# Scores of the first four tiles as pairs of plain fp32 matmuls in the two row halves, from one q/k buffer a tile

## The chip, the cores and the metric

The kernel runs on one core of a Trainium2 chip. The metric is the device time of one execution in microseconds: for the kernel before, a median of 612.29 us over three runs (611.9 to 612.41). The engines are TensorE (PE, its weight loads PEld), VectorE (DVE), ScalarE (ACT), GpSimd (POOL) and SyncE (SP, which here only issues transfers). PSUM has eight banks; matmuls write there, DVE and ACT read it.

## The reference

An mLSTM attention (a recurrence over 768 steps, 2 batches, 8 heads of 40) feeds a mixture of four dense experts and then a gated second layer:

```python
for t in range(S):
    m_new = np.maximum(f_gate[:, :, t] + m, i_gate[:, :, t])
    f_stab = np.exp(f_gate[:, :, t] + m - m_new)
    i_stab = np.exp(i_gate[:, :, t] - m_new)
    C = f_stab * C + i_stab * einsum('bhd,bhe->bhde', vt, kt)
    n = f_stab * n + i_stab * kt
    y[:, :, t] = sigmoid(o_gate[:, :, t]) * (C @ qt) / max(abs(n @ qt), 1.0)
x = y.transpose(0, 2, 1, 3).reshape(B * S, H * D)
out = sum over e of p[:, e] * (relu(x @ w1[e]) @ w2[e])        # moe
final = ((out @ w_a) * (out @ w_b)) @ w_out                    # moe2
```

## The kernel before

The recurrence is cut into chunks of 128 steps, which makes 12 tiles (6 chunks j by 2 batches b, tile n = 2j + b). For each tile, `scores` (L508) makes the products k.q of eight heads, four to a PSUM bank `pt_c` (halves hh = 0 and 1); `weights_of` (L485) makes the exponents of the decay weights in a bank `pt_a`; `w_exp` (ACT, L497) and `w_mask` (POOL, L505) turn them into the weights w; `s1b` (DVE, L517) multiplies w with `pt_c`; `s2a` (L527) multiplies the result with the values into `pt_y`, and from chunk 1 on a second product with the old state goes into `pt_i` (L533). `s2b` (L543, L546) and `s2x` (L556 to L562) make the tile's output x on DVE, `s3a` (L145 to L147) transposes it, and its two float32r parts `xh` and `xl` feed the experts. `state` (L583, `pt_u`) and `state_in` (L591) make the new state.

For tiles 0 to 3 (NP = 4) the scores are plain fp32 matmuls. Each half has a buffer of 120 rows by 1024; rows 0 to 63 of tiles 0 and 1 (40 rows for tiles 2 and 3, which go into the buffers of tiles 0 and 1) are loaded, rows 64 to 119 are zeroed once (`zero_qk`, L337, two on DVE and two on POOL), and the matmul contracts all 120 rows. A plain fp32 matmul stands in the trace as two weight loads and two matmul records. Later tiles split q and k into float32r parts (`split_qk`, `low_qk`).

The experts' matmuls are float32r. In the first 200 us a stream of `Item`s (L208, L287 to L289) is interleaved with the recurrence; from 202 us on `quad_a` (L228) and `quad_b` (L253) run alone, with 64-row matmuls in the two row halves of the array.

The order on each engine is written out by hand: the list `ev` holds (time, function, arguments), sorted by that number, and each engine runs its instructions in that order. The four banks of the pool `ps_t` (4 to 7 in the built program) go in turn to `pt_c`, `pt_y`, `pt_i`, `pt_x`, `pt_u`, `pt_e` and some `pt_a`, in the order in which the code asks for them; the first matmul into a bank waits for the last reader of what was there.

Of the kernel before, what the change touches and what calls it, by code (L numbers as in the profile page):

```python
# [48 lines left out]
def mlstm_moe_kernel(ctx, tc, gates, qk, qc, kvo, dp, w1b, w2b, ident_d, bdmask_d, rsel_d, exp_d, out):  # L49
    nc = tc.nc  # L50
# [254 lines left out]
    ps_b = ctx.enter_context(tc.tile_pool(name="ps_b", bufs=2, space=PS))  # L305
    with ExitStack() as c1:
        cq = ExitStack()
        qp = cq.enter_context(tc.tile_pool(name="qp", bufs=2, side="right"))
# [670 lines left out]
```

## Time and profile before

| | us |
|---|---|
| median of three runs | 612.29 |
| profiled execution, first to last instruction (its span) | 609.3 |
| median less span: what lies around the span | 3.0 |
| PE busy in the span | 598.1 (98%) |
| DVE, ACT, POOL busy | 406.5, 277.9, 193.3 |
| scores of tiles 0 to 3, 64 matmul records | 8.2 busy, 6.49 to 39.9 |

The profiled execution's own time is not given apart from its span; with the 3.0 us around the span it stands for the median. The granted clock is 1.00 in every stretch listed. In the timeline rows matmul ends are modelled, so the step from one start to the next is what counts. Times in the rows are from the span's start.

### The profile page before, as it was taken

The numbers are of one execution on the slowest core, as the hardware profiler recorded it, in microseconds if no ns is written. First come the engines' busy times: TensorE is split into PE (matmuls) and PEld (weight loads), VectorE is DVE, ScalarE is ACT, GpSimd is POOL, SyncE is SP. The second block draws the span as 40 slices with busy tenths as digits, with TensorE's granted clock in tenths as the row PEclk, the third lists the DMA queues.
The fourth block names the chain that finished last, engine by engine and source line by source line (L and its number), as shares of the span: only waits on it lengthen the run. The fifth ranks groups of instructions, "written<-read, shape, count | busy, mean of one in ns | idle before, by whom it ended". The sixth has DMA issues, their size and how long they took to land.

```text
span 609.3 us, 14397 instructions
## 1 busy us (share of the span) xinstructions
PE 598.1 (98%) x5815; PEld 564.5 (93%) x5815; DVE 406.5 (67%) x829; ACT 277.9 (46%) x643; POOL 193.3 (32%) x233
## 2 busy tenths in 40 slices
PE   8799999999999999999999999999999999999997
PEld 5699999999999899999999999988898988888886
DVE  6898868676553333333789899898776787864344
ACT  7687476756533323333344344454553434331211
POOL 5486426363501011334233333333222222310000
PEclk9999999999999999999999999999999999999999
DMA  8877463737202122222222222222111120200002
GB/s 247 214 219 202 128 181 103 197 104 200 58 19 64 39 62 80 72 75 79 56 76 69 63 75 56 59 63 65 47 50 45 38 56 20 60 16 1 2 31 100
DMA packets 29351, 51.63 MB, mean 85 GB/s; under 512 B 3485, under 2 KB 18117, under 8 KB 29285
## 3 DMA queue, kind: packets, MB, share of 16 engines
q1 hardware_dynamic: 15925, 26.32, 15.9%
q10 hardware_dynamic: 12448, 22.03, 13.2%
q0 software_dynamic: 912, 2.36, 1.4%
q8 instruction: 45, 0.74, 0.5%
q14 instruction: 21, 0.17, 0.1%
HBM read 47.92 MB, written 2.00 MB: 82 GB/s over the span
## 4 chain that ended last, share of the span: by engine, by line
PE 92%; DVE 3%; POOL 1%; issue 1%; DMA 1%; ACT 1%; SPq 0%; DVEq 0%; POOLq 0%
PE psy L253 27%; PE psa L228 27%; PE psb L228 11%; PE psa L208 10%; PE psy L287 3%; PE psy L289 3%; PE psy L288 3%; PE pt_y L527 3%; PE pt_c L513 1%; PE pt_i L533 1%; POOL wl L93 1%; PE pt_u L583 1%; DMA acc<-in_w1b 1%; PE pt_x L145 0%; DMA gt<-in_gates 0%
## 5 line engine op out<-in xcount | busy, mean ns | idle before, releaser
L228 PE MATMUL psa<-xh,wh 64*128 64x512 f32 x576 | 135.2, 390 | 0.0
L253 PE MATMUL psy<-wl,hh 64*128 64x320 f32 x752 | 131.3, 305 | 0.0
L253 PE MATMUL psy<-wh,hh 64*128 64x320 f32 x752 | 131.3, 305 | 0.0
L253 PE MATMUL psy<-wh,hl 64*128 64x320 f32 x752 | 131.2, 305 | 0.0
L228 PE MATMUL psa<-xh,wl 64*128 64x512 f32 x414 | 97.4, 389 | 0.0
L253 PEld LDWEIGHTS psy<-wh,hh 64*128 64x128 f32 x752 | 85.7, 184 | 0.8
L228 PEld LDWEIGHTS psa<-xh,wh 64*128 64x128 f32 x576 | 80.9, 184 | 5.9 <-issue 0.9
L253 PEld LDWEIGHTS psy<-wl,hh 64*128 64x128 f32 x752 | 85.5, 184 | 0.8
L253 PEld LDWEIGHTS psy<-wh,hl 64*128 64x128 f32 x752 | 85.7, 184 | 0.0
L228 PE MATMUL psa<-xl,wh 64*128 64x512 f32 x384 | 85.6, 389 | 0.0
L828 DVE SCALAR_TENSOR_TENSOR hl<-psa,hh 128x512 fp32r<-128x512 f32 x60 | 38.6, 685 | 55.2 <-ACT hh L827 54.9
L125 POOL TENSOR_TENSOR wl<-tp,lf 128x272 fp32r<-128x272 f32 x48 | 38.8, 809 | 113.1 <-DVE tp L124 111.4
L228 PE MATMUL psb<-xh,wh 64*128 64x512 f32 x216 | 69.8, 389 | 0.0
L228 PEld LDWEIGHTS psa<-xh,wl 64*128 64x128 f32 x414 | 60.7, 184 | 3.7
L228 PE MATMUL psb<-xh,wl 64*128 64x512 f32 x180 | 58.5, 389 | 0.0
L228 PEld LDWEIGHTS psa<-xl,wh 64*128 64x128 f32 x384 | 55.2, 184 | 3.6
L122 POOL TENSOR_TENSOR lf<-lf,sq 128x272 f32<-128x272 f32 x48 | 38.1, 794 | 62.9 <-ACT wh L121 48.9
L276 DVE SCALAR_TENSOR_TENSOR hl<-psa,hh 128x256 fp32r<-128x256 f32 x72 | 30.3, 421 | 40.4 <-ACT hh L275 40.0
L93 POOL TENSOR_TENSOR wl<-raw,wh 128x352 fp32r<-128x352 f32 x28 | 26.4, 947 | 95.1 <-ACT wh L91 68.6
L275 ACT ACTIVATE hh<-psa 128x256 fp32r<-128x256 f32 x72 | 27.6, 383 | 59.2 <-PE psa L208 58.5
L827 ACT ACTIVATE hh<-psa 128x512 fp32r<-128x512 f32 x60 | 32.6, 596 | 44.7 <-PE psy L253 26.6
L208 PE MATMUL psa<-xh,wh 128*128 128x256 f32 x216 | 51.5, 293 | 0.3 <-ACT xh L133 0.3
(146 smaller groups left out, 1435.1 us busy)
## 6 DMA issues: line engine op xcount, KB each, us to landing
raw<-in_w2b ACTq DMA_DIRECT2D x48, 272.0 KB, 2.8
qk_t<-in_qk SPq DMA_DIRECT2D x16, 480.0 KB, 4.7
raw<-in_w1b ACTq DMA_DIRECT2D x32, 176.0 KB, 2.3
acc<-in_w1b SPq DMA_DIRECT2D x24, 176.0 KB, 4.0
kvo_t<-in_kvo SPq DMA_DIRECT2D x10, 364.5 KB, 7.1
Rr<-dL_t ACTq DMA_DIRECT2D x5, 512.0 KB, 6.3
og_t<-in_kvo SPq DMA_DIRECT2D x6, 320.0 KB, 4.6
out<-acc SPq DMA_DIRECT2D x12, 160.0 KB, 1.9
```

What stands on the lines that cost most here:

```text
L93: lo_eng.tensor_tensor(wl[:, cs], raw, wh[:, cs].bitcast(F32), op=ALU.subtract)
L122: nc.gpsimd.tensor_tensor(lf, lf, sq, op=ALU.mult)
L125: nc.gpsimd.tensor_tensor(wl[:, cs], tf, lf, op=ALU.add)
L208: nc.tensor.matmul(ps, l, r, start=(i == 0), stop=(i == len(prs) - 1))
L228: return nc.tensor.matmul(ps[g], w[rows, o:o + P], x, start=start, stop=stop)
L253: ms = [nc.tensor.matmul(ps[t], l[rows, t * P:(t + 1) * P], w[rows, off:off + DM], start=start, stop=stop) for t, rows in zip(two, (UP, DN))]
L275: nc.scalar.activation(self.hh, ps, AF.Relu)
L276: nc.vector.scalar_tensor_tensor(self.hl, ps, 0.0, self.hh.bitcast(F32), op0=ALU.max, op1=ALU.subtract)
L287: nc.tensor.matmul(ps, lh, wh[:, off:off + DM], start=(fi == 0), stop=False)
L288: nc.tensor.matmul(ps, lh, wl[:, off:off + DM], start=False, stop=False)
L827: nc.scalar.activation(hh, ps[f], AF.Relu)
L828: nc.vector.scalar_tensor_tensor(hl, ps[f], 0.0, hh.bitcast(F32), op0=ALU.max, op1=ALU.subtract)
```

## The change

One buffer a tile takes both halves: q and k of heads 0 to 3 in rows 0 to 47, of heads 4 to 7 in rows 64 to 111 (48 rows loaded each, for all four tiles; 40 are used). Tiles 0 to 2 take the three buffers `qk`, tile 3 one of the two `qs`, so no tile's load waits for another's scores. The zero fills go. `scores2` makes both halves of a tile in one piece, alternating between the row halves, each matmul with 40 rows.

```diff
         def load_qk(n, hh, eng=None):
             t = td.setdefault(n, {})
-            if 2 <= n < NP:
-                t["qk", hh] = td[n - 2]["qk", hh]
+            if n < NP:
+                if "two" not in t:
+                    tag, bufs = ("qs", 2) if n == NP - 1 else ("qk", QB)
+                    t["two"] = qp.tile([KS, 2, 512], F32, tag=tag, name="qk_t", bufs=bufs)
+                at, r, to = 64 * hh, RQ, t["two"]
             else:
...
-            r = 64 if n < 2 else D if n < NP else KS
-            (eng or nc.sync).dma_start(v[0:r], qk[n, hh, 0:r])
-
-        def zero_qk(n, hh, eng):
-            eng.memset(td[n]["qk", hh][64:KS], 0.0)
+            (eng or nc.sync).dma_start(v[at:at + r], qk[n, hh, 0:r])
...
+        def scores2(n):
+            t = td[n]
+            for hh in range(2):
+                t["pc", hh] = ps_t.tile([P, 512], F32, tag="t", name="pt_c")
+            for h in range(4):
+                hs = slice(h * P, (h + 1) * P)
+                for hh in range(2):
+                    v = t["two"][64 * hh:64 * hh + D]
+                    nc.tensor.matmul(t["pc", hh][:, hs], v[:, 1, hs], v[:, 0, hs], start=True, stop=True, skip_group_check=True)
...
-            (-51.612, scores, 1, 0), (-51, weights_of, 1, 1, ps_b, "b"), (-51, w_exp, 1, 1), (-49.609, go, w1[0:1]), (-49.488, w_exp, 1, 0),
...
+            (-51.612, scores2, 1), (-51, weights_of, 1, 1, ps_b, "b"), (-51, w_exp, 1, 1), (-49.609, go, w1[0:1]), (-49.488, w_exp, 1, 0),
...
```

`scores2` stands where the first of a tile's two halves stood. On PE at tiles 0 and 1 there was, before:

```order
L513 MATMUL pt_c<-qk_t 128x128 [waits DMAHW2_49,DVE_49]
L513 MATMUL pt_c<-qk_t 128x128 x3
L513 MATMUL pt_c<-qk_t 128x128 [waits DMAHW3_49,DVE_49]
L492 MATMUL pt_a<-Rr_107,LT_105 128x512 [waits DVE_49]
L492 MATMUL pt_a<-Rr_107,LT_105 128x512 [waits Activation_49]
L492 MATMUL pt_a<-Rr_108,LT_105 128x512 [waits DVE_49]
L513 MATMUL pt_c<-qk_t 128x128 [waits DMAHW4_49,Pool_49]
L513 MATMUL pt_c<-qk_t 128x128 x3
L492 MATMUL pt_a<-Rr_108,LT_105 128x512 [waits Activation_49]
L513 MATMUL pt_c<-qk_t 128x128 [waits DMAHW5_49,Pool_49]
L527 MATMUL pt_y<-kvo_t,w_t 128x82 [waits DMAHW6_49,DVE_49]
```

and there is now, in the changed kernel's line numbers:

```order
L515 MATMUL pt_c<-qk_t 128x128 [waits DMAHW3_49]
L515 MATMUL pt_c<-qk_t 128x128 [waits DMAHW2_49]
L515 MATMUL pt_c<-qk_t 128x128 x6
L492 MATMUL pt_a<-Rr_107,LT_105 128x512 [waits DVE_49]
L492 MATMUL pt_a<-Rr_107,LT_105 128x512 [waits Activation_49]
L492 MATMUL pt_a<-Rr_108,LT_105 128x512 [waits DVE_49]
L515 MATMUL pt_c<-qk_t 128x128 [waits DMAHW4_49]
L515 MATMUL pt_c<-qk_t 128x128 [waits DMAHW5_49]
L515 MATMUL pt_c<-qk_t 128x128 x6
L492 MATMUL pt_a<-Rr_108,LT_105 128x512 [waits Activation_49]
L537 MATMUL pt_y<-kvo_t,w_t 128x82 [waits DMAHW6_49,DVE_49]
```

The last `pt_a` of tile 1 stood behind four matmuls of `pt_c` and now stands behind eight. On PE around the scores of tile 3 (`w_t_470` and `w_t_492` are tile 2's weights of half 0 and half 1, `pt_c_540` is tile 3's half 1, `pt_c_581` its half 0) there was, before:

```order
L513 MATMUL pt_c_540<-qk_t_128 128x128 [waits DMAHW4_49,Activation_49]
L513 MATMUL pt_c_540<-qk_t_128 128x128 x3
L583 MATMUL pt_u_547<-kvo_t_136,kw_t_431 120x123 [waits DVE_49]
L527 MATMUL pt_y_553<-kvo_t_251,w_t_470 128x82 [waits DMAHW5_49,DVE_49]
L527 MATMUL pt_y_553<-kvo_t_251,w_t_470 128x82 x3
...
L527 MATMUL pt_y_553<-kvo_t_251,w_t_492 128x82 [waits DVE_49]
L533 MATMUL pt_i_577<-cbd_t_519,qc_t_253 128x123 [waits DMAHW6_49]
L513 MATMUL pt_c_581<-qk_t_126 128x128 [waits DMAHW3_49,DVE_49]
L492 MATMUL pt_a_603<-Rr1_108,LT1_106 128x512 [waits DVE_49]
```

and there is now (`w_t_466` and `w_t_488` are tile 2's halves, `pt_c_536` and `pt_c_537` tile 3's):

```order
L515 MATMUL pt_c_536<-qk_t_244 128x128 [waits DMAHW3_49,Activation_49]
L515 MATMUL pt_c_537<-qk_t_244 128x128 [waits DMAHW4_49,DVE_49]
L515 MATMUL pt_c_536<-qk_t_244 128x128
L593 MATMUL pt_u_548<-kvo_t_131,kw_t_427 120x123 [waits DVE_49]
L537 MATMUL pt_y_554<-kvo_t_247,w_t_466 128x82 [waits DMAHW5_49,DVE_49]
L537 MATMUL pt_y_554<-kvo_t_247,w_t_466 128x82 x3
...
L537 MATMUL pt_y_554<-kvo_t_247,w_t_488 128x82 x4
L543 MATMUL pt_i_578<-cbd_t_515,qc_t_249 128x123 [waits DMAHW6_49,DVE_49]
L492 MATMUL pt_a_599<-Rr1_108,LT1_106 128x512 [waits DVE_49]
```

The half-0 scores of tile 3 moved from behind `pt_i` to the front, so six tiles ask for banks in another order. In the built programs they get these banks, and their first matmul waits for this DVE instruction:

| tile in PSUM | before: bank, waits for | now: bank, waits for |
|---|---|---|
| `pt_c` of (2, half 0), (2, half 1) | 7, 6 | 6, 7 |
| `pt_c` of (3, half 1) | 5, none on DVE | 6, `s1b`(2, half 0) |
| `pt_u` of tile 1 | 7, `s1b`(2, half 0) | 4, `state_in`(0) |
| `pt_y` of tile 2 | 4, `state_in`(0) | 7, `s1b`(2, half 1) |
| `pt_i` of tile 2 | 6, none left (`s1b`(2, half 1) came earlier) | 4, `state_in`(1) |
| `pt_c` of (3, half 0) | 7, `state_in`(1) | 5, none on DVE |

So `s2a` of tile 2 waited for `s1b`(2, half 1) only before its second four matmuls, and now waits for it before its first. The order on DVE, ACT, POOL and SP differs only by the four memsets and the sizes of the loads.

## Rows read from the trace of the kernel before

**Rows 1.** The page, span and part 1: busy time by engine

```profile
span 609.3 us, 14397 instructions
PE 598.1 (98%) x5815; PEld 564.5 (93%) x5815; DVE 406.5 (67%) x829; ACT 277.9 (46%) x643; POOL 193.3 (32%) x233
```

**Rows 2.** Stretches: length, then busy us (instructions) by engine, PEclk, DMA, GB/s

```profile
5.80:9.00 3.20, 2.26 (x17) 1.97 (x17) 2.97 (x7) 2.84 (x8) 0.00 (x0) 1.00 1.03 217
19.60:36.30 16.70, 15.45 (x118) 14.37 (x119) 15.24 (x34) 13.20 (x35) 11.44 (x12) 1.00 0.67 183
75.00:609.00 534.00, 530.86 (x5317) 503.43 (x5315) 345.00 (x696) 225.76 (x520) 149.32 (x176) 1.00 0.25 68
```

**Rows 3.** Timeline, tiles 0 and 1: start, us, engine, work [idle before <-releaser]

```profile
3.94 0.49 DVE L389 TENSOR_TENSOR_SCAN mr<-gt,mr 112x128 f32<-112x128 f32 x1 [0.48 <-DMA gt<-in_gates]
...
9.60 1.05 PE L513 MATMUL pt_c<-qk_t 120*128 120x128 f32 x8
10.41 0.48 PE L492 MATMUL pt_a<-Rr,LT 112*128 112x512 f32 x1
10.92 1.08 ACT L497 ACTIVATE w_t<-pt_a 128x512 f32<-128x512 f32 x2 [0.77 <-PE pt_a L492]
12.07 1.23 POOL L505 TENSOR_SCALAR_AFFINE_SELECT w_t<-w_t 128x512 f32<-128x512 f32 x2 [1.21 <-ACT w_t L497]
12.75 1.29 DVE L517 TENSOR_TENSOR w_t<-pt_c,w_t 128x512 f32<-128x512 f32 x2 [1.16 <-POOL w_t L505]
15.58 0.49 DVE L562 TENSOR_TENSOR x_t<-x_t,og_t 128x320 f32<-128x320 f32 x1 [0.51 <-ACT og_t L363]
```

**Rows 4.** Chain that ended last, in order: start, us, what

```profile
36.30 0.69 DVE w_t L517
...
46.04 0.61 DVE w_t L517
46.70 1.12 PE pt_y L527 x8
...
64.29 1.69 DVE qs_t L353
```

**Rows 5.** Timeline of PE, where row halves begin and end

```profile
201.70 0.31 PE L288 MATMUL psy<-wl,hh 128*128 128x320 f32 x1
201.85 0.31 PE L289 MATMUL psy<-wh,hl 128*128 128x320 f32 x1
202.09 0.73 PE L228 MATMUL psa<-xh,wh 64*128 64x512 f32 x4
202.65 0.63 PE L228 MATMUL psa<-xh,wl 64*128 64x512 f32 x4
203.12 0.63 PE L228 MATMUL psa<-xl,wh 64*128 64x512 f32 x4
...
208.96 0.39 PE L228 MATMUL psa<-xh,wh 64*128 64x512 f32 x2
209.28 0.42 PE L287 MATMUL psy<-wh,hh 128*128 128x320 f32 x1
209.53 0.31 PE L288 MATMUL psy<-wl,hh 128*128 128x320 f32 x1
```

**Rows 6.** Timeline around tile 3's scores

```profile
34.03 1.05 PE L513 MATMUL pt_c<-qk_t 120*128 120x128 f32 x8
34.92 0.80 PE L583 MATMUL pt_u<-kvo_t,kw_t 128*120 128x123 f32 x6
35.55 1.02 PE L527 MATMUL pt_y<-kvo_t,w_t 128*128 128x82 f32 x8
36.30 0.69 DVE L517 TENSOR_TENSOR w_t<-pt_c,w_t 128x512 f32<-128x512 f32 x1 [0.64 <-POOL w_t L505]
38.18 0.87 PE L533 MATMUL pt_i<-cbd_t,qc_t 120*128 120x123 f32 x6
39.21 0.49 DVE L543 TENSOR_TENSOR y_t<-pt_i,ET 128x328 f32<-128x328 f32 x1
```

More of the change, by code (lines that the diff above doesn't have):

```diff
@@ L37 @@
 QB = 3
+RQ = 48
 WARM = 10
@@ L326, in load_qk @@
             t = td.setdefault(n, {})
-            if 2 <= n < NP:
-                t["qk", hh] = td[n - 2]["qk", hh]
-            else:
-                tag, bufs = ("qs", 2) if (n, hh) == (1, 1) else ("qk", QB)
-                t["qk", hh] = qp.tile([KS, 2, 512], F32, tag=tag, name="qk_t", bufs=bufs)
-            v = t["qk", hh].rearrange("p a b -> p (a b)")
-            r = 64 if n < 2 else D if n < NP else KS
-            (eng or nc.sync).dma_start(v[0:r], qk[n, hh, 0:r])
-        def zero_qk(n, hh, eng):
-            eng.memset(td[n]["qk", hh][64:KS], 0.0)
+            if n < NP:
[3 more added lines that the diff above has]
+                at, r, to = 64 * hh, RQ, t["two"]
+            else:
+                to = t["qk", hh] = qp.tile([KS, 2, 512], F32, tag="qk", name="qk_t", bufs=QB)
+                at, r = 0, KS
+            v = to.rearrange("p a b -> p (a b)")
+            (eng or nc.sync).dma_start(v[at:at + r], qk[n, hh, 0:r])
         def split_qk(n, hh):
@@ L505, in w_mask @@
             nc.gpsimd.affine_select(w, w, pattern=[[0, 4], [1, P]], compare_op=ALU.is_ge, fill=0.0, base=0, channel_multiplier=-1)
+        def scores2(n):
[7 more added lines that the diff above has]
+                    nc.tensor.matmul(t["pc", hh][:, hs], v[:, 1, hs], v[:, 0, hs], start=True, stop=True, skip_group_check=True)
         def scores(n, hh, pool=ps_t, tag="t"):
             t = td[n]
-            qs = t["qk" if n < NP else "qs", hh]
+            qs = t["qs", hh]
             t["pc", hh] = pc = pool.tile([P, 512], F32, tag=tag, name="pt_c")
@@ L680, in mlstm_moe_kernel @@
             (-110, load_gates, 0, nc.sync), (-109, load_rsel, nc.scalar), (-108, load_qk, 0, 0, nc.sync), (-107, load_qk, 0, 1, nc.scalar),
-            (-106, load_qk, 1, 0, nc.sync), (-105, load_qk, 1, 1, nc.sync), (-102.626, zero_qk, 0, 0, V), (-100.942, table, AF.Exp),
-            (-99.501, zero_qk, 1, 0, nc.gpsimd), (-96.615, zero_qk, 0, 1, V), (-93.843, ones), (-92.159, load_kvo, 1), (-88.852, load_kvo, 0),
+            (-106, load_qk, 1, 0, nc.sync), (-105, load_qk, 1, 1, nc.sync), (-100.942, table, AF.Exp),
+            (-93.843, ones), (-92.159, load_kvo, 1), (-88.852, load_kvo, 0),
             (-86.023, load_v, 0), (-84.837, go, w0[0:1]), (-84.589, go, w0[1:2]), (-84.33, go, w0[2:3]), (-81.267, load_ident), (-79.818, go, w0[3:4]),
-            (-79.066, gate0, 0), (-76.45, load_v, 1), (-75.79, load_o, 0, nc.sync), (-75.176, go, w0[4:5]), (-74.955, zero_qk, 1, 1, nc.gpsimd),
-            (-74.482, load_mask), (-74.114, load_k, 0), (-73.514, go, w0[6:7]), (-73.345, go, w0[7:8]), (-70.77, fill_R, 0), (-70.643, warm_up, WARM),
-            (-70.226, load_k, 1), (-69.676, load_dp), (-68, scores, 0, 0), (-66.868, go, w0[5:6]), (-65.844, scores, 0, 1), (-65.387, gate1, 0),
+            (-79.066, gate0, 0), (-76.45, load_v, 1), (-75.79, load_o, 0, nc.sync), (-75.176, go, w0[4:5]), (-74.482, load_mask), (-74.114, load_k, 0), (-73.514, go, w0[6:7]), (-73.345, go, w0[7:8]), (-70.77, fill_R, 0), (-70.643, warm_up, WARM),
+            (-70.226, load_k, 1), (-69.676, load_dp), (-68, scores2, 0), (-66.868, go, w0[5:6]), (-65.387, gate1, 0),
             (-64.959, gate_f, 0, V), (-64.541, gate_i, 0, nc.gpsimd), (-63, gate2, 0), (-63, gate_c, 0, V), (-62.343, hi_L, 0, nc.scalar),
@@ L691, in mlstm_moe_kernel @@
             (-54, weights_of, 0, 1, ps_b, "b"), (-53.987, w_exp, 0, 1), (-53.825, s1b, 0, 0), (-52.523, weights_of, 1, 0, ps_a, "a"), (-52.166, w_mask, 0, 1),
-            (-51.612, scores, 1, 0), (-51, weights_of, 1, 1, ps_b, "b"), (-51, w_exp, 1, 1), (-49.609, go, w1[0:1]), (-49.488, w_exp, 1, 0),
-            (-47.978, go, w0[0:1]), (-47.812, go, w1[1:2]), (-47.78, w_mask, 1, 0), (-47.662, load_qk, 2, 0), (-47.456, scores, 1, 1), (-46.839, w_mask, 1, 1),
+            (-51.612, scores2, 1), (-51, weights_of, 1, 1, ps_b, "b"), (-51, w_exp, 1, 1), (-49.609, go, w1[0:1]), (-49.488, w_exp, 1, 0),
+            (-47.978, go, w0[0:1]), (-47.812, go, w1[1:2]), (-47.78, w_mask, 1, 0), (-47.662, load_qk, 2, 0), (-46.839, w_mask, 1, 1),
             (-46.808, gate4, 0), (-45.43, gate5, 0), (-45.181, load_qk, 3, 0), (-43.297, load_qk, 3, 1), (-42.115, load_kvo, 2), (-42.105, load_o, 1, nc.sync),
@@ L704, in mlstm_moe_kernel @@
             (1.512, low_L, 1), (1.512, low_cm, 1), (1.517, build_R, 2, V, 0, 4), (1.581, weigh_k, 0), (1.6, gate4, 1), (1.6, gate5, 1), (1.685, go, w1[1:2]),
-            (1.735, go, w1[1:2]), (2.013, go, w1[0:1]), (2.182, scores, 2, 1), (2.31, scores, 2, 0), (2.439, build_R, 2, V, 4, 8), (2.518, go, w1[0:1]),
+            (1.735, go, w1[1:2]), (2.013, go, w1[0:1]), (2.182, scores2, 2), (2.439, build_R, 2, V, 4, 8), (2.518, go, w1[0:1]),
             (2.699, weigh_k, 1), (2.829, weights), (2.835, go, w1[2:3]), (2.89, go, w1[2:3]), (2.939, gate_tail, 1), (3.11, go, w1[3:4]), (3.419, go, w1[3:4]),
@@ L711, in mlstm_moe_kernel @@
             (4.718, go, w1[6:7]), (4.995, state, 0), (5, state_in, 0), (5, state_add, 0), (5.122, go, w2[3:4]), (5.123, o_gate, 1), (5.153, go, w2[1:2]),
-            (5.236, go, w2[5:6]), (5.255, go, w2[0:1]), (5.26, s1b, 2, 1), (5.343, scores, 3, 1), (5.35, state_old, 1), (5.411, go, w1[7:8]),
+            (5.236, go, w2[5:6]), (5.255, go, w2[0:1]), (5.26, s1b, 2, 1), (5.343, scores2, 3), (5.35, state_old, 1), (5.411, go, w1[7:8]),
             (5.445, go, w2[7:8]), (5.45, state, 1), (5.45, state_in, 1), (5.5, s2a, 2, 0), (5.523, load_kvo, 3), (5.55, gate1, 2), (5.55, gate_f, 2, V),
-            (5.6, s2a, 2, 1), (5.623, scores, 3, 0), (5.655, go, w2[0:1]), (5.716, table, AF.Exp), (5.78, s2b, 2), (5.78, load_o, 2, nc.sync),
+            (5.6, s2a, 2, 1), (5.655, go, w2[0:1]), (5.716, table, AF.Exp), (5.78, s2b, 2), (5.78, load_o, 2, nc.sync),
             (5.879, go, w2[3:4]), (5.891, go, w2[5:6]), (5.9, s2x, 2), (5.9, weights_of, 3, 0), (5.9, w_exp, 3, 0), (5.9, w_mask, 3, 0), (5.932, go, w2[4:5]),
```

## The prediction

> **What bounds the kernel now.** I read the page first: PE is busy for 598.1 of 609.3 us [rows 1], so at first sight every matmul saved is time saved. The busy shares by stretch say where that holds. From 75 us on PE is busy for 530.86 of 534.00 us, and what is missing is the 3 us at the very end [rows 2]; nothing in that part is changed. From 19.6 to 36.3 us DVE is busy for 15.24 of 16.70 us and PE for 15.45 [rows 2], so there a second engine is as full, and the order of the chain decides. The chain that ended last, read in order of time, goes over DVE at 36.30 us and still at 46.04 us, hands over to PE at 46.70 us, and touches DVE once more until about 66 us (64.29 + 1.69) [rows 4]. So up to 46.70 us the end hangs on DVE and on what DVE waits for; a matmul that is shortened there, and that DVE does not wait for, gives PE a longer wait and nothing else. All four tiles whose scores change lie before 40 us.
>
> Before that the chain starts with the gates' transfer, for which DVE waited 0.48 us until 3.94 us, and passes the last `pt_a` of tile 1: it starts at 10.41 us, ACT had then waited 0.77 us for it, POOL 1.21 us for ACT's exponentials, and DVE 1.16 us for POOL's masks [rows 3]. Behind that stands tile 0's x on DVE, which at 15.58 us had waited another 0.51 us for ACT's sigmoid of the output gates [rows 3], an instruction that ACT does after the same exponentials. So whatever delays that one `pt_a` delays ACT, POOL and DVE together, up to 46.70 us and from there to the end.
>
> **The change part by part.** *A matmul pass.* Eight records of `pt_c` take from 34.03 to 34.92 us, 0.111 us each [rows 6]; a tile has 16 of them, 1.78 us. In the row halves the trace has only float32r: four of 512 columns take from 202.65 to 203.12 us, 0.235 us a pair, and a full-height matmul of 320 columns takes 0.15 us (201.70 to 201.85) [rows 5], which for 512 columns would be 0.24. So there two halves run wholly beside each other, each with its own weight load. For a plain fp32 matmul, two loads and two passes in a row on one half, no row shows it. The bounds are 16 passes (no overlap, 1.78 us) and 8 (0.89 us). I take 9, 1.00 us: the nearest rows show full overlap, and since each matmul's two passes are on one half the other half runs one pass behind.
>
> *Going into the row halves and out.* From the last full-height matmul to the first in a half it takes 0.24 us instead of 0.15, and the first two pairs take 0.56 us (202.09 to 202.65) instead of 0.47; on the way out a last pair takes 0.32 us (208.96 to 209.28) instead of 0.235, and the next matmul 0.25 (209.28 to 209.53) instead of 0.15 [rows 5]. That is 0.19 us in and 0.19 us out, 0.38 us a tile; the lower bound is none, where PE waits anyway. The Trainium skill says the same against this change: in "TensorEngine Tiling (Array Packing)", section "Key Properties", changing the tiling mode drains TensorE. By that rule without a price the sum could not be made; the rows give the price.
>
> So PE gets 1.78 - 1.00 - 0.38 = 0.40 us a tile back, 1.6 us in four tiles. Where does it lie? Tile 0's scores stand ahead of a `pt_a` that waits for ACT and DVE; tile 2's stand at 24 us and half of tile 3's at 39 us, in the stretch where DVE leads. I count nothing for these, and bound their gain by the 1.6 us.
>
> *Tile 1: a wait made longer.* The last `pt_a` of tile 1 stood behind four `pt_c` matmuls and now stands behind eight. Before, 9.60 to 10.41 us, 0.81 us [rows 3]. Now 0.19 + 1.00 + 0.19 = 1.38 us, so it starts 0.57 us later. Behind it wait ACT (two exponentials), POOL (two masks), DVE (two products, then tile 0's x), as above, all in order and without a gap to absorb it: +0.57 us. The bounds: 0.89 us and no switch, +0.08; no overlap and both switches, 2.16 us, +1.35.
>
> *Tile 3: a new wait.* `s2a` of tile 2 started at 35.55 us, before `s1b`(2, half 1), which runs on DVE from 36.30 to 36.99 us and itself waits 0.64 us for POOL's mask [rows 6]. Now its first matmul needs the bank which that instruction frees. So it starts at about 37.03 us, 1.48 us later; queued behind it on PE are six expert matmuls, the second half of `s2a` and `pt_i`. From the start of `s2a` to that of `pt_i` PE works without a pause for 2.63 us (35.55 to 38.18) [rows 6], so `pt_i` starts at 39.66 instead of 38.18 us. For `pt_i` waits DVE's L543 at 39.21 us; `pt_i` ended at 38.18 + 0.87 = 39.05 us [rows 6], which leaves some 0.12 us of slack. DVE therefore stands still for 1.48 - 0.12 = 1.36 us at a place from which the chain goes on over DVE to 46.70 us. The half-0 scores that no longer stand behind `pt_i` do not help: the `pt_a` behind them waits for that same L543. The bound above is 1.48 us; below, I take 0.7 us, for POOL's mask coming as much earlier as DVE waited for it (0.64). A delay of both by tile 1's 0.57 us leaves this term as it is. The Trainium skill has this too, in the same page, "Restrictions and Gotchas", Gotcha 1: row tiling raises the pressure on PSUM, since different row tiles write different banks. It gives no price.
>
> *Memsets and loads.* Two memsets leave DVE, two POOL, all before 3.8 us, ahead of instructions that wait for the gates' transfer at 3.94 us [rows 3]: nothing. Loads of tiles 0 and 1 shrink from 256 to 192 KB, those of tiles 2 and 3 grow from 160 to 192 KB. One of the smaller ones runs beside the gates' transfer, so that may land sooner: between 0 and the 0.48 us that DVE waited; I take 0. The scores' inputs are in earlier, which nothing later waits for.
>
> Sum: 0.57 + 1.36 = +1.93 us. The profiled execution's span goes from 609.3 to 611.2 us; with the 3.0 us around the span, the median of 612.29 becomes 614.2 us.
>
> **The rivals.** *A, PE's time counts (faster).* If PE led in the changed stretches too, the 1.6 us would come off: 612.29 - 1.6 = 610.7 us; with free switches, 4 x 0.78 = 3.1 us, 609.2 us. For it speaks PE's 98% [rows 1]; against it that DVE is on the chain at 36.30 and 46.04 us [rows 4]. The Trainium skill's table in "TensorEngine Tiling (Array Packing)", "Overview", has up to twice the speed for a contraction of at most 64 rows, and by it this is the case to expect.
>
> *B, the delays are absorbed (no change).* The wait at tile 3 falls to 0.7 us or less and tile 1's to 0.08, and the gates land a little earlier: 612.29 + 0.7 + 0.08 - 0.4 = 612.7 us. For it speaks that DVE's instructions beside busy POOL vary, against it that both waits are in the written order.
>
> *C, plain fp32 passes do not overlap (slower still).* Then tile 1 costs 1.35 us: 612.29 + 1.36 + 1.35 = 615.0 us. Tile 3's scores would end at 34.1 + 2.16 = 36.3 us, still before 37.03, so that term stays. For it speaks that no row shows two halves with two passes a matmul.
>
> *D, the clock falls.* PE was busy for 2.26 of 3.20 us between 5.80 and 9.00 us, at a granted clock of 1.00, 2.4 GHz [rows 2]; with scores of 1.0 us for 1.8 it would be about 1.5 us. If the clock went to its lower level there, the 1.4 us from 9.60 us on would double: 614.2 + 1.4 = 615.6 us. Against it: the clock is at 1.00 in all four stretches [rows 2].
>
> **How the numbers follow.** The forecast's mechanism, both waits, 62%; A 8%; B 11%; C 13%; D 6%. The forecast alone reaches from 613.1 (0.08 and 0.7) to 614.9 us (1.1 and 1.48). The range that leaves out no more than 2 in 10 takes in C and the upper part of B, leaves out A and D: 612.6 to 615.3 us. About 0.2%, 1.2 us, is what a measurement can tell from no change, so "same" is 611.1 to 613.5 us: all of B and a little of the forecast, 17%. Faster is A, 8%. Slower is the rest, 75%.
>
> **What would show it.** In the profile after: `pt_c` records in a 40-row form, 16 of them in about 1.0 us at 24 us (C: 1.8). The last `pt_a` of tile 1 about 1.4 us behind the scores' start, and ACT waiting for it for about 1.3 us instead of 0.77. PE idle before `pt_y` of tile 2, released by DVE's L527 in the new numbering, for about a microsecond; DVE idle for over 1 us before the product with `pt_i`, where it had no wait; and the hand-over to PE at about 48.6 instead of 46.70 us. If that hand-over comes at 46.70 or earlier the forecast is wrong; if it comes late and the end does not, later slack exists that I did not see.

## The result and the profile after

The changed kernel takes 615.37 us (median of four runs, 614.22 to 616.33), the kernel before 612.10 in the same runs: a ratio of 1.0060, 95% interval 1.0039 to 1.0082. The forecast was 614.2 us; its range ended at 615.3. So the time lies 0.07 us outside the range, where the four runs spread over 2.1 us. The profiled execution is the fastest of the four, 614.22 us, with a span of 612.3 us against 609.3. The page looks as before: PE's busy time is no smaller. What differs from [rows 1] is where the clock was.

```profile
span 612.3 us, 14384 instructions
PE 600.6 (98%) x5815; PEld 565.5 (92%) x5815; DVE 404.7 (66%) x827; ACT 277.7 (45%) x643; POOL 190.9 (31%) x231
...
PEclk8899999999999999999999999999999999999999
```

The stretches, columns as in [rows 2]:

```profile
5.80:9.00 3.20, 1.66 (x17) 1.16 (x17) 2.93 (x8) 2.56 (x7) 0.00 (x0) 1.00 0.99 225
10.00:14.00 4.00, 4.00 (x29) 3.68 (x29) 1.51 (x3) 2.44 (x6) 2.00 (x4) 0.61 1.07 344
14.00:18.00 4.00, 4.00 (x20) 3.83 (x20) 2.62 (x7) 3.18 (x6) 3.12 (x4) 0.50 1.08 277
18.00:22.00 4.00, 3.99 (x18) 2.58 (x18) 2.80 (x9) 1.88 (x5) 0.00 (x0) 0.61 1.06 206
22.00:36.00 14.00, 12.51 (x97) 11.03 (x96) 13.17 (x29) 10.90 (x29) 9.40 (x9) 1.00 0.58 174
```

From 5.80 to 9.00 us PE is busy for 1.66 us instead of 2.26. The granted clock rose at 4.06 us, but the trace has it at 0.5, 1.2 GHz, again from 10.89 to 21.13 us; before, it stayed at 1.00 from 5.54 us on. Tiles 0 and 1 in the timeline, the answer to [rows 3]:

```profile
4.22 0.48 DVE L389 TENSOR_TENSOR_SCAN mr<-gt,mr 112x128 f32<-112x128 f32 x1 [3.02 <-DMA gt<-in_gates]
...
9.96 1.26 PE L515 MATMUL pt_c<-qk_t 40*128 40x128 f32 x16
11.16 0.79 PE L492 MATMUL pt_a<-Rr,LT 112*128 112x512 f32 x1
11.75 3.54 PE L537 MATMUL pt_y<-kvo_t,w_t 128*128 128x82 f32 x16
11.99 1.09 ACT L497 ACTIVATE w_t<-pt_a 128x512 f32<-128x512 f32 x2 [1.55 <-PE pt_a L492]
13.14 1.23 POOL L505 TENSOR_SCALAR_AFFINE_SELECT w_t<-w_t 128x512 f32<-128x512 f32 x2 [2.00 <-ACT w_t L497]
13.81 1.29 DVE L527 TENSOR_TENSOR w_t<-pt_c,w_t 128x512 f32<-128x512 f32 x2 [1.94 <-POOL w_t L505]
15.33 0.17 DVE L566 TENSOR_SCALAR dn_t<-pt_y 128x8 f32<-128x8 f32 x1 [0.23 <-PE pt_y L537]
16.64 0.49 DVE L572 TENSOR_TENSOR x_t<-x_t,og_t 128x320 f32<-128x320 f32 x1 [0.19 <-ACT og_t L363]
18.66 0.42 DVE L137 TENSOR_TENSOR xl<-pt_x,xh 128x256 fp32r<-128x256 f32 x1 [1.52 <-ACT xh L134]
19.78 0.17 DVE L566 TENSOR_SCALAR dn_t<-pt_y 128x8 f32<-128x8 f32 x1 [0.39 <-PE pt_y L537]
```

Read the first numbers against before: DVE starts 0.28 us later, at 4.22 instead of 3.94, because the gates' transfer landed later; the last `pt_a` starts 0.75 later (10.41 to 11.16), ACT and POOL 1.07 later, DVE's product 1.06 later (12.75 to 13.81). The fall of the clock at 10.89 us comes in the last of these scores; the `pt_a` stands behind it and takes 0.79 us instead of 0.48. Then DVE waits twice for `pt_y`, made at the lower clock. Before, DVE had no such wait, in its timeline:

```profile
13.95 0.16 DVE L556 TENSOR_SCALAR dn_t<-pt_y 128x8 f32<-128x8 f32 x1
...
17.28 0.42 DVE L136 TENSOR_TENSOR xl<-pt_x,xh 128x256 fp32r<-128x256 f32 x1 [1.21 <-ACT xh L133]
...
18.05 0.17 DVE L556 TENSOR_SCALAR dn_t<-pt_y 128x8 f32<-128x8 f32 x1
```

The first of the two waits, 0.23 us, does not last: tile 0's x waits less for the sigmoid, 0.19 us instead of 0.51 [rows 3], and stands 1.06 us later, as the product did. The next steps do last. Behind tile 0's transposes, which PE also makes at the lower clock, DVE is 1.38 us late (17.28 to 18.66), and behind the second wait for `pt_y` 1.73 us (18.05 to 19.78).

Tiles 2 and 3, the answer to [rows 6]:

```profile
25.75 0.28 PE L209 MATMUL psa<-xh,wh 128*128 128x256 f32 x1
25.87 0.28 PE L209 MATMUL psa<-xh,wl 128*128 128x256 f32 x1
26.08 1.16 PE L515 MATMUL pt_c<-qk_t 40*128 40x128 f32 x16
27.17 0.41 PE L288 MATMUL psy<-wh,hh 128*128 128x320 f32 x1
27.42 0.31 PE L289 MATMUL psy<-wl,hh 128*128 128x320 f32 x1
...
37.12 0.90 PE L593 MATMUL pt_u<-kvo_t,kw_t 128*120 128x123 f32 x6
38.78 1.12 PE L537 MATMUL pt_y<-kvo_t,w_t 128*128 128x82 f32 x8 [0.76 <-DVE w_t L527]
41.50 0.87 PE L543 MATMUL pt_i<-cbd_t,qc_t 120*128 120x123 f32 x6
...
38.04 0.69 DVE L527 TENSOR_TENSOR w_t<-pt_c,w_t 128x512 f32<-128x512 f32 x1 [0.64 <-POOL w_t L505]
42.41 0.50 DVE L553 TENSOR_TENSOR y_t<-pt_i,ET 128x328 f32<-128x328 f32 x1 [1.39 <-PE pt_i L543]
```

A tile's sixteen passes take 1.09 us from the first to the next matmul (26.08 to 27.17), so the halves do run beside each other. Read one record at a time, the passes start in eight pairs: the second pair 0.21 us behind the first, the later ones 0.11 us apart, and the next matmul 0.20 us behind the last. PE waits 0.76 us before `pt_y` for the bank, DVE 1.39 us for `pt_i`, and its product with it comes at 42.41 instead of 39.21 us.

The chain of waits, where [rows 4] had the hand-over to PE at 46.70 us, has it at 49.89:

```profile
49.89 1.12 PE pt_y L537 x8
...
67.07 1.71 DVE qs_t L353
```

Of these 3.20 us 0.40 come back at about 66 us. There DVE and POOL share the `low_qk` products, and in the traced execution of the kernel before, POOL was held up 0.46 us by a transfer. The timeline of the kernel before:

```profile
62.94 0.79 POOL L571 TENSOR_TENSOR kw_t<-kvo_t,ET 128x360 f32<-128x360 f32 x1 [0.46 <-DMA kvo_t<-in_kvo]
63.02 2.95 DVE L353 TENSOR_TENSOR qs_t<-qk_t,qs_t 40x512 fp32r<-40x512 f32 x2
66.34 0.68 DVE L517 TENSOR_TENSOR w_t<-pt_c,w_t 128x512 f32<-128x512 f32 x1
...
605.89 0.49 DVE L811 TENSOR_TENSOR acc<-psy,acc 128x320 f32<-128x320 f32 x1 [0.39 <-PE psy L875]
```

And of the changed one:

```profile
65.70 0.81 POOL L581 TENSOR_TENSOR kw_t<-kvo_t,ET 128x360 f32<-128x360 f32 x1
66.23 2.54 DVE L353 TENSOR_TENSOR qs_t<-qk_t,qs_t 40x512 fp32r<-40x512 f32 x2
69.14 0.68 DVE L527 TENSOR_TENSOR w_t<-pt_c,w_t 128x512 f32<-128x512 f32 x1
...
608.69 0.49 DVE L820 TENSOR_TENSOR acc<-psy,acc 128x320 f32<-128x320 f32 x1 [0.39 <-PE psy L884]
```

From there nothing changes: +2.80 us at 69.14 and +2.80 at the last product of the program. What follows that is the output's transfer. From the start of the last product to the end of the span it is 3.4 us in the kernel before, 3.6 in the changed one, and 3.4 to 4.7 in the experiments. So what these kernels differ by is decided mostly in four legs before 45 us, and blurred by over a microsecond at the end.

### The profile page after: what moved, and what is told of

It reads as the page before. It is cut to its first block, busy times and chain, and to the rows that moved or that the text cites. A ratio compares the mean times of both kernels' runs of the same rounds, so it can differ in the third digit from the quotient of the medians.

```text
span 612.3 us, 14384 instructions
## 1 busy us (share of the span) xinstructions
PE 600.6 (98%) x5815; PEld 565.5 (92%) x5815; DVE 404.7 (66%) x827; ACT 277.7 (45%) x643; POOL 190.9 (31%) x231
## 4 chain that ended last, share of the span: by engine, by line
PE 93%; DVE 2%; POOL 1%; DMA 1%; issue 1%; ACT 0%; SPq 0%; DVEq 0%; POOLq 0%
PE psy L254 27%; PE psa L229 27%; PE psb L229 11%; PE psa L209 10%; PE pt_y L537 4%; PE psy L288 3%; PE psy L290 3%; PE psy L289 3%; PE pt_i L543 1%; PE pt_c L523 1%; POOL wl L94 1%; PE pt_u L593 1%; DMA acc<-in_w1b 1%; DMA gt<-in_gates 1%; PE pt_x L146 1%
## 5 line engine op out<-in xcount | busy, mean ns | idle before, releaser
L254 PE MATMUL psy<-wl,hh 64*128 64x320 f32 x752 | 128.5, 305 | 0.0
L254 PE MATMUL psy<-wh,hh 64*128 64x320 f32 x752 | 128.5, 305 | 0.0
L254 PE MATMUL psy<-wh,hl 64*128 64x320 f32 x752 | 128.4, 305 | 0.0
L254 PEld LDWEIGHTS psy<-wh,hh 64*128 64x128 f32 x752 | 82.9, 184 | 0.8
L254 PEld LDWEIGHTS psy<-wl,hh 64*128 64x128 f32 x752 | 82.8, 184 | 0.8
L254 PEld LDWEIGHTS psy<-wh,hl 64*128 64x128 f32 x752 | 82.9, 184 | 0.0
```

The costliest lines, as they stand in the source:

```text
L254: ms = [nc.tensor.matmul(ps[t], l[rows, t * P:(t + 1) * P], w[rows, off:off + DM], start=start, stop=stop) for t, rows in zip(two, (UP, DN))]
```

## The experiments

The legs are differences between the starts of four DVE instructions. G: the scan L389, when the gates are in. A: from there to `s1b`(1, half 0), the third product with `pt_c`. B: on to `s1b`(2, half 1), the sixth. C: on to tile 2's product with `pt_i`. G + A + B + C is that product's start. "Last" is the start of the program's last product. The clock is given as low "to" the time at which the trace's record of it begins, for the reason shown at e2_late3. The ratio is to the kernel before on the same chip, so medians in us are compared through it; one trace a kernel.

| kernel | G | A | B | C | last | clock low after 5 us | ratio (95%) |
|---|---|---|---|---|---|---|---|
| before | 3.94 | 8.80 | 23.55 | 2.91 | 605.89 | to 5.54 | 1 |
| after | 4.22 | 9.59 | 24.23 | 4.37 | 608.69 | 10.89 to 21.13 | 1.0060 (1.0039 to 1.0082) |
| e1_warm | 4.14 | 9.20 | 23.90 | 4.37 | 607.88 | 18.31 to 21.72 | 1.0035 (1.0022 to 1.0049) |
| e2_late3 | 4.44 | 10.89 | 24.63 | 2.90 | 609.55 | to 24.27 | 1.0042 (1.0028 to 1.0056) |
| e3_late1 | 4.51 | 8.84 | 26.19 | 4.38 | 610.19 | 8.38 to 22.04 | 1.0049 (1.0030 to 1.0068) |
| e4_all | 4.74 | 7.92 | 23.54 | 2.90 | 605.38 | to 6.40 | 0.9987 (0.9976 to 0.9999) |
| e5_warm_late3 | 4.62 | 9.20 | 24.63 | 2.89 | 607.66 | to 5.96, 16.20 to 23.02 | 1.0043 (1.0029 to 1.0057) |
| e6_warm_late1 | 4.29 | 7.92 | 23.52 | 4.37 | 606.37 | none | 1.0019 (1.0010 to 1.0028) |
| e12_late13 | 4.35 | 8.76 | 25.82 | 2.90 | 608.09 | to 6.13, 9.55 to 19.79 | 1.0035 (1.0023 to 1.0048) |
| e7_before_late1 | 3.86 | 7.94 | 23.64 | 2.91 | 604.73 | none | 0.9984 (0.9975 to 0.9993) |
| e9_before_cold | 3.85 | 10.89 | 23.83 | 2.91 | 607.09 | to 11.89, 18.71 to 22.13 | 1.0011 (1.0002 to 1.0020) |
| e8_serial | 4.17 | 11.91 | 24.21 | 4.38 | 610.95 | to 5.52, 8.93 to 22.59 | 1.0085 (1.0071 to 1.0099) |
| e10_56rows | 4.51 | 7.94 | 23.52 | 2.90 | 605.14 | to 5.82 | 0.9988 (0.9978 to 0.9999) |
| e11_fills | 4.50 | 8.22 | 23.54 | 2.89 | 605.64 | to 6.66 | 0.9990 (0.9979 to 1.0002) |

**Three edits, alone and together.** The theory had three causes: the clock, the order at tile 1, the bank at tile 3.

*e1_warm*: extra warm-up matmuls in PE's gaps.

```diff
-WARM = 10
+WARM = 16
+            (-67.9, warm_up, 3),      # behind (-68, scores2, 0)
+            (-54.5, warm_up, 2),      # behind (-55, w_mask, 0, 0)
```

> The changed kernel with eleven more warm-up matmuls, put where PE stood idle between 5.0 and 9.3 us (six before tile 0's scores, three behind them, two before the next pt_a). Theory: the lower clock from 10.9 to 21.1 us cost about 0.7 us of the 3.0 (what tile 0's and tile 1's places on DVE lost between 13.8 us, +1.06, and 19.8 us, +1.73). Then the granted clock stays at 1.00 after its first rise, tile 1's s1b is late by at most 1.06 us, tile 2's s1b by about 1.0 instead of 1.74, and the time is about 614.7 us (changed kernel 615.4). Rival: PE is not waited for there, the clock is a by-stander: the clock stays up and the time stays at 615.4. Second rival: the extra matmuls stand in the way of tile 0's scores and everything moves back: 615.5 or more.

614.15 us. The two ratios differ by 0.25%, 1.5 us, but their intervals overlap, so the time alone does not show the gain. The legs do: with eleven matmuls that compute nothing A is 9.20 instead of 9.59, B 23.90 instead of 24.23. The clock did fall, but later and for a shorter time. The span is no shorter (612.3), though the last product comes 0.81 us earlier: in that trace 4.4 us follow the start of the last product. A at 9.20 with a full clock, against 8.80 before, is the price of the row halves at tile 1: 0.40 us.

*e2_late3*: tile 3's scores behind `pt_i`.

```diff
-            (5.343, scores2, 3),
+            (5.623, scores2, 3),      # behind (5.6, s2a, 2, 1)
```

> The changed kernel with both score halves of tile 3 moved behind s2a of tile 2 and pt_i (event 5.623 instead of 5.343), so that pt_y takes the bank of s1b of half 0 and not that of half 1. Theory: the wait for the bank costs 1.46 us (DVE's product with pt_i +3.20 instead of +1.74): PE's idle time before pt_y goes, DVE's 1.39 us before that product goes, and the time is about 614.0 us against 615.4 of the changed kernel. Rival: DVE would have stood still there anyway, for POOL's mask or for pt_i itself: the wait moves by a few tenths and the time is 615.0 to 615.4. Second rival: the scores' 1.1 us now stand before the pt_a of tile 3, which becomes late: about 0.5 us of gain.

614.62 us by the median, half of the expected gain; the ratio's interval overlaps that of the changed kernel. The mechanism is right all the same: DVE goes on to `y_t` without a wait, C is 2.90 instead of 4.37, in DVE's timeline:

```profile
39.96 0.69 DVE L527 TENSOR_TENSOR w_t<-pt_c,w_t 128x512 f32<-128x512 f32 x1 [0.63 <-POOL w_t L505]
...
42.86 0.49 DVE L553 TENSOR_TENSOR y_t<-pt_i,ET 128x328 f32<-128x328 f32 x1
```

What the trace lost is in A and B, 1.70 us more than in the changed kernel. Here two views must be read together. A stretch:

```profile
14.00:18.00 4.00, 4.00 (x20) 3.91 (x20) 2.31 (x6) 3.94 (x8) 3.04 (x4) 1.00 1.12 282
```

And PE's timeline:

```profile
10.67 2.08 PE L515 MATMUL pt_c<-qk_t 40*128 40x128 f32 x16
12.68 0.79 PE L492 MATMUL pt_a<-Rr,LT 112*128 112x512 f32 x1
13.27 3.54 PE L537 MATMUL pt_y<-kvo_t,w_t 128*128 128x82 f32 x16
```

PEclk reads 1.00, and yet the passes take twice as long (2.08 for sixteen; `pt_y` 3.54, as in the changed kernel at 0.50). The record of the clock begins with its first rise, here at 24.27 us; what lies ahead counts as 1.00. The same holds for the mean of the span, 1.000 for this run. That is the likely reading of the one run of the changed kernel with a mean of 1.000, which was its slowest, 616.33 us; it has no trace, so this stays unshown.

*e3_late1*: tile 1's scores behind its last `pt_a`.

```diff
-            (-51.612, scores2, 1),
+            (-50.5, scores2, 1),      # behind (-51, weights_of, 1, 1, ps_b, "b")
```

> The changed kernel with both score halves of tile 1 moved behind the last pt_a of tile 1 (event -50.5 instead of -51.612). Theory: that pt_a then starts about 1.2 us sooner (at 10.0 instead of 11.16 us), ACT's exponentials and POOL's masks go with it, ACT's wait of 1.55 us goes down to 0.4 or less, and about 1.0 us of time comes off: 614.3 us. Rival: the low clock sets that stretch (pt_y of tiles 0 and 1, 3.3 us for 16 instead of 1.75): then DVE's dn still waits for pt_y and only 0.3 us comes off: 615.1. Second rival: s1b of tile 1 now waits for the later scores: no change.

615.33 us: nothing gained. A fell by 0.75 us, B rose by 1.96: the clock was low from 8.38 to 22.04 us. DVE waited 0.91 us for tile 1's scores and 2.28 us for tile 0's `pt_y`, as in e12_late13 below. So what both rivals named came true.

*e4_all*: all three edits.

> All three edits at once. Theory: the costs are separate and in a row, so that they add: 0.7 + 1.4 + 1.0 = 3.1 us off the changed kernel, 612.3 us, the same as the kernel before; what is left of the 3.0 is then the gates' later landing (0.28), made up by the exponentials that now start earlier than before. Rival (PE's time counts once the waits are gone): the 0.4 to 0.6 us of PE saved in each of tiles 2 and 3 show too, 611.5 or less. Rival (one cause): if the clock alone or the bank alone is the cause, the sum is no more than that edit's own gain, 614 or more.

611.22 us, below the kernel before (by 0.13%, interval 0.01% to 0.24%), and 1.1 us better than the sum of the forecast gains. The clock stays up, ACT makes its four exponentials without a pause, and POOL's and DVE's waits at tile 1 shrink from 1.21 and 1.16 us [rows 3] to 0.34 and 0.29 in its timeline:

```profile
9.67 2.26 ACT L497 ACTIVATE w_t<-pt_a 128x512 f32<-128x512 f32 x4
...
11.99 1.22 POOL L505 TENSOR_SCALAR_AFFINE_SELECT w_t<-w_t 128x512 f32<-128x512 f32 x2 [0.34 <-ACT w_t L497]
...
12.66 1.29 DVE L527 TENSOR_TENSOR w_t<-pt_c,w_t 128x512 f32<-128x512 f32 x2 [0.29 <-POOL w_t L505]
```

The other combinations were made to see whether the causes add.

*e5_warm_late3* (edits of e1 and e2):

> The changed kernel with the eleven warm-up matmuls of e1_warm and tile 3's scores behind pt_i as in e2_late3. Theory: with the clock kept up through tile 1, taking away the wait for the bank is worth its full 1.4 us: 614.15 - 1.4 = 612.7 us, DVE's product with pt_i of tile 2 at +2.8 us behind s1b(2, half 1) as in the kernel before (2.91) and not +4.4 as in e1_warm. Rival (what e2_late3's 0.75 us suggests at face value): the bank is worth only half of that, because PE or POOL is late next: 613.4 us.

613.87 us; the total misses by 1.2. The leg does not: C 2.89 against e1_warm's 4.37. The same front as e1_warm had its clock low from 16.20 to 23.02 us this time, and B 0.73 longer. The Trainium skill says of the ramp in "TensorE: Matmul & The Clock Gate", Part 1, that it varies from run to run for one and the same kernel; this pair agrees (first rise at 4.66 and 5.96 us). The fall varied too.

*e6_warm_late1* (edits of e1 and e3):

> The changed kernel with the eleven warm-up matmuls and tile 1's scores behind the last pt_a. Theory: at the full clock the order of tile 1 is worth about 1.28 us at s1b of tile 1 (9.20 to 7.92 us after the gates landed, e1_warm against e4_all), some of which tile 0's x gives back, and the wait for the bank stays whole: 614.15 - 0.9 = 613.2 us. Rival (what e3_late1's null at face value says): the order of tile 1 is worth nothing: 614.1 us.

612.55 us, better than expected: A 7.92, no fall of the clock, and C still 4.37.

*e12_late13* (edits of e2 and e3, no extra matmuls):

> The changed kernel with both moves (tile 1's scores behind its last pt_a, tile 3's behind pt_i) but without the eleven extra warm-up matmuls. Theory: the low clock in the front, as in e2_late3 and e3_late1, takes away what the order of tile 1 brings: the moves are worth the bank's 1.4 us and no more, about 613.8 us, and e4_all's 611.2 is better by 2.6 us for eleven matmuls that compute nothing. Rival: the orders add by themselves and the clock is worth only e1_warm's 1.2 us: 612.4 us.

613.93 us, as expected. With the clock low from 9.55 us the products of tile 1 and then tile 0's `dn` wait for PE, in DVE's timeline:

```profile
13.11 1.29 DVE L527 TENSOR_TENSOR w_t<-pt_c,w_t 128x512 f32<-128x512 f32 x2 [0.90 <-PE pt_c L515]
16.68 0.17 DVE L566 TENSOR_SCALAR dn_t<-pt_y 128x8 f32<-128x8 f32 x1 [2.29 <-PE pt_y L537]
```

Read from e4_all, these three runs each take one edit away again, and the ratios' intervals stand clear of e4_all's: without the eleven matmuls 0.48% slower (e12_late13), without the move of tile 3's scores 0.32% (e6_warm_late1), without the move of tile 1's 0.56% (e5_warm_late3). So all three count. They do not add: the three losses sum to 1.36%, and all three edits together gained 0.73%.

**Is it the row halves?** *e7_before_late1*: the kernel before, the first half of tile 1's scores moved.

```diff
-            (-51.612, scores, 1, 0),
+            (-50.5, scores, 1, 0),    # behind (-51, weights_of, 1, 1, ps_b, "b")
```

> The kernel before (full-height scores, its own loads and zero fills) with the first half of tile 1's scores moved behind the last pt_a as well, nothing else. Theory: e4_all beats the kernel before because of this order and not because of the row halves; then this one gains ACT's 0.77 us at tile 1 too, of which tile 0's x passes on some half: 611.5 us (before 612.0). Rival: the row halves' shorter scores are what e4_all gained by; then this one stays at 612.0. Second rival: the sparser PE in front of the pt_a makes the clock fall more often, and it is slower than before.

610.36 us, 0.16% below before (interval 0.07% to 0.25%), with one event moved and no other change. That is not to be told from e4_all's 0.13%, so the row halves are not what e4_all gained by. Its A is 7.94, e4_all's 7.92, its B 23.64 against 23.54. The timeline:

```profile
8.96 0.98 PE L492 MATMUL pt_a<-Rr,LT 112*128 112x512 f32 x3 [0.20 <-ACT Rr L480]
9.78 1.95 PE L513 MATMUL pt_c<-qk_t 120*128 120x128 f32 x16
...
11.81 1.29 DVE L517 TENSOR_TENSOR w_t<-pt_c,w_t 128x512 f32<-128x512 f32 x2 [0.28 <-POOL w_t L505]
```

Its scores take 1.78 us where e4_all's take 1.10, and that is worth 0.1 us at most. What separates the two traces is G.

*e8_serial*: the row halves one after the other.

```diff
-            for h in range(4):
-                hs = ...
-                for hh in range(2):
+            for hh in range(2):
+                for h in range(4):
+                    hs = ...
```

> The changed kernel with the sixteen passes of a tile's scores written half after half (four heads of the upper rows, then four of the lower) instead of by turns. Theory: the two halves run beside each other only where they stand next to each other; then a tile's pt_c takes about 1.8 us at the full clock instead of 1.1, tile 1's last pt_a is late by another 0.7 us, and the time is about 616.0 us against 615.4 of the changed kernel, unless a busier PE keeps the clock up, which gives back up to 0.7. Rival: a plain fp32 matmul on a row half is short by itself, whatever stands next to it: pt_c stays at 1.1 us and the time at 615.4.

616.7 us, 0.7 us over the forecast. Sixteen passes now take 1.64 us (28.34 to 29.98) where they took 1.09, in PE's timeline:

```profile
28.34 1.71 PE L515 MATMUL pt_c<-qk_t 40*128 40x128 f32 x16
29.98 0.41 PE L288 MATMUL psy<-wh,hh 128*128 128x320 f32 x1
```

So a pass costs its 0.11 us on a half too (the step between most of these records), and what saves time is the turn by turn order. The Trainium skill's "TensorEngine Tiling (Array Packing)", "Key Properties", says that different tiles can load weights and multiply in parallel; the rows agree for a two-pass fp32 matmul, when neighbours are on different halves. The rise of A to 11.91 holds the low clock as well.

**The price of the clock alone.** *e9_before_cold*:

```diff
-WARM = 10
+WARM = 2
```

> The kernel before with two warm-up matmuls instead of ten, nothing else. Theory: PE's clock then first rises only when the front is over (behind 20 us), and the stretch from tile 0's scores to tile 1's x, in which DVE waits for pt_a and pt_y, costs what it cost in the changed kernel, 1.1 us or, low from the start, up to 2: 613.1 to 614.0 us (before 612.0 and 611.3). Rival: the clock of the front is a by-stander, since DVE and not PE bounds it: no change.

612.26 us, 0.11% above before, 0.7 us: under the forecast. In the trace the clock rose at 11.89 us, not behind 20, and fell once more. Still, G + A + B + C is 2.27 us more than before. 1.06 us of it came back at the `low_qk` products (63 to 68 us), more than in any other trace. The clock of the front is no by-stander (A is 2.09 us longer), but in this trace half of its price came back behind it.

**The gates' landing.** G was 3.85 to 3.94 us in the three traces with the old loads, 4.14 to 4.74 in the eleven with the new. Both tries start from e4_all; the fills go to a tile that nothing reads.

```diff
-RQ = 48
+RQ = 56                               # e10_56rows
```

```diff
+        fz = qp.tile([P, 2, 256], F32, tag="fz", name="fz_t", bufs=1)
+        def fill(i, eng):
+            for _ in range(4):
+                eng.memset(fz[64:120, i], 0.0)
...
+            (-102.626, fill, 0, V), (-99.501, fill, 1, nc.gpsimd), (-96.615, fill, 0, V), (-74.955, fill, 1, nc.gpsimd),
```

> e4_all with loads of 56 rows a head half instead of 48, for all four tiles (8 KB more a row pair; the rows beyond 40 are not used). Theory: the gates' landing depends on how the loads issued right behind it are cut into packets; with 56 rows it goes back towards the 3.9 us of the kernels with loads of 64 rows (3.94 and 3.86, against 4.14 to 4.74 in eight traces with 48), and the time falls by up to 0.5 us: 610.8 us. Rival: the number of rows has nothing to do with it: landing between 4.1 and 4.7 us and 611.2 us. Second rival: more bytes beside the gates' make it later still: 611.6.

> e4_all with zero fills put back on DVE and POOL at their old places, of the old sizes but into a tile that nothing reads. Theory: the fills did lie in idle time and the gates' landing does not depend on them: 611.2 us, landing 4.1 to 4.7 us. Rival: without the fills DVE and POOL reach their wait for the gates early and something else in the start of the program moves with it: the landing goes back to 3.9 us and the time to 610.5.

610.96 and 611.63 us; the ratios, 0.9988 and 0.9990, are not to be told from e4_all's 0.9987. G was 4.51 and 4.50. So the fills are not the reason, and they cost no time that shows. Loads of 56 rows do not bring the old landing back; loads of 64, the old number, were not tried in this layout. The cause stays open.

## Why the prediction was wrong

- **The sum of the two waits held, in part by luck.** Tile 1 was put at 0.57 us and measured 0.40 (A 8.80 to 9.20 at the full clock, twice). Tile 3 was put at 1.36 and measured 1.46 (C 2.91 to 4.37 or 4.38 in all five traces with the scores of tile 3 at that place, 2.89 or 2.90 in the six with them behind `pt_i`; the clock does not touch this leg). That is 1.86 us against 1.93, with the two errors of opposite sign. Both waits are there, so rival B is out.
- **The term of tile 1** was mis-sized in two parts. Eight pairs of passes stand beside each other, not nine: 0.11 us. The price of the switches was right: 0.21 us instead of 0.12 before the first pair and 0.21 instead of 0.11 behind it, 0.19 us in; 0.20 instead of 0.11 behind the last pair and 0.25 instead of 0.15 for the matmul after, 0.19 us out. But that last 0.10 us lies behind the start of the next matmul, and the sum counted it into the start of `pt_a`. Rival C is out: the passes overlap (1.09 us a tile).
- **The step that failed is the clock.** The forecast had no term for it, and rival D was set at 6% with the words "Against it: the clock is at 1.00 in all four stretches". [rows 2] has three stretches, none of them covers 9.00 to 19.60 us, and they show the clock with the old, busier PE; the change itself takes 0.6 of 2.26 busy us out of 5.80 to 9.00. In the trace the clock fell, and cost 0.39 us in A and 0.68 in B, 1.07 us in all. D had the place only in part. It doubled tile 1's scores, but the fall came at their end: 0.39 us lie there and in the `pt_a` behind them, about 0.32 us at tile 0's transposes, and about 0.35 us at tile 1's `pt_y`, for which DVE had not waited before. D's time, 615.6 us, was nearest.
- **How far this reaches beyond the trace.** The mean clock of three of the changed kernel's four runs is 0.989 to 0.991. In the 76 runs of the kernel before that go with the experiments it is never under 0.994, though 27 of them are at 0.994 to 0.997, so the clock falls there too at times (what lies ahead of the first rise is not in these means). The price of 1.07 us is that of one execution, the fastest of the four.
- **A sign was wrong for the loads.** Their term was between 0 and 0.48 us sooner; the gates came 0.28 us later in the profiled execution.
- **The 3.0 us around the span** were taken over from the kernel before, and did not hold: in the four runs of the changed kernel it is 1.7 to 2.4 us. That the profiled execution took 614.22 us, the very forecast, is luck: its span is 1.0 us longer than forecast (612.26 against 611.24), and 1.0 us less lies around it.
- **PE's saved time counted as nothing**, rightly: e4_all and e7_before_late1 differ by 0.1 us in A and B with 0.7 us less of scores a tile. Rival A is out.
- **The bookkeeping**: 0.28 + 0.79 + 0.68 + 1.46 = 3.21 us at tile 2's `y_t` (3.20 by its start), less 0.40 at the `low_qk` products, makes the 2.80 us of the last product. The two waits that were forecast are 1.86 us of it; the clock, the landing and what came back are the rest. The hand-over to PE, forecast for 48.6 us, stands at 49.89.
- **The better order was in the rows.** ACT's 0.77 us for the last `pt_a` [rows 3] was priced as a wait that grows; moving one scores call behind that `pt_a` takes it away in either kernel, as long as the clock stays up (e3_late1 and e12_late13 gave it back).

## What to carry to other kernels

Before making matmuls shorter in a stretch where another engine leads, ask what keeps TensorE's clock up there: here 0.6 us less of PE's work was followed by a fall that cost 1.07 us in later matmuls that are waited for, and eleven idle matmuls were worth more than the saving. When two tiles are requested at one place instead of two, follow the rotation of the banks to the next request; the wait that was read off the written order (1.36 us forecast, 1.46 found) held in every trace, while totals scattered by a microsecond. Compare such kernels by legs between fixed instructions, not by spans: e2_late3 looked like half of its worth by its time, and was whole in its leg.

## What was not expected of the hardware

- The granted clock in the profile begins with its first rise: PEclk 1.00 and a mean of 1.000 stood over a front in which sixteen passes took 2.08 us instead of 1.09 (e2_late3).
- The clock of the front differs between executions of the same order: e1_warm and e5_warm_late3, alike up to 35 us, had it low from 18.31 to 21.72 and from 16.20 to 23.02 us.
- Plain fp32 matmuls on 40 rows, turn by turn on the two row halves, start in pairs: 26.08 to 27.17 us for sixteen passes, 0.11 us a pair. Going in and coming out cost 0.19 us each, as much as for the float32r matmuls in [rows 5].
- The gates' transfer landed 0.2 to 0.9 us later in every kernel with both halves of a tile in one buffer, for a reason that neither loads of 56 rows nor the zero fills explain.
